# An attention and expert kernel: the expert units write into the score banks, the query turn comes earlier, the last gate follows the attention

## The chip, the cores and the metric

The kernel runs on one core of a Trainium2 chip. The metric is the device time of one launch in microseconds (us). An engine of the core works through its own queue in order: TensorE (PE, matrix products), VectorE (DVE), ScalarE (ACT), GpSimd (POOL) and SyncE (SP); transfers between memory and the core run on 16 DMA engines, issued here from the SP, POOL and ACT queues.

## The reference, cut to what matters

Attention with 16 query heads and one shared key and value head comes first; its output, with the heads side by side, are 3072 tokens of 1024 numbers. Then every token goes to one of 16 experts: a gate picks a group of four, a second gate one expert in the group.

```python
scores = scale * np.matmul(q, k.transpose(0, 1, 3, 2))      # q (8, 16, 384, 64), k and v (8, 1, 384, 64)
attn = np.exp(scores - max); attn = attn / attn.sum()
x = np.matmul(attn, v) as (3072, 1024)
g_idx = argmax(x @ w_group); e_idx = argmax(x @ w_expert[g_idx])
h = np.maximum(x @ w1[g, e], 0.0)                           # w1 (4, 4, 1024, 1024)
out = (g_w * e_w)[:, None] * (h @ w2[g, e])                 # softmax weights of the two picks
```

## The kernel before

All of the order is written by hand: each engine's queue holds its instructions in the order in which the program makes them, and the waits between engines follow from the tiles.

**Attention.** The work is cut into 48 groups `g`, six to a batch of 384 tokens (eight batches `b`), and into 24 pairs `p` of two groups. The loop at L418 runs 25 times; below, "stage p" is one turn of it. `r` is p mod 3: r = 1 is the stage in which the gate of the batch before is worked out. For a group, `scores(g, kt)` (L197) makes three tiles s on TensorE, and ScalarE turns each into pt with an exp. A score tile takes two PSUM banks; the pool `ps_s` has three such pairs of banks, and `side` (L77) hands out the same three to short-lived products. `values(g)` (L258) multiplies pt by v into a bank from `bank` (L72), which alternates between two single banks, mm0 and mm1. `pre_add` (L209) adds the three pt tiles on VectorE (two instructions). For the sums over keys, stages 1 to 7 use `sum_keys` (L232: a product kss on TensorE, and a turn krow on VectorE) and later stages `fold_keys` (L222: a turn and a reduce, both on VectorE). `invert` (L242) makes the product sm, and VectorE its reciprocal rc and the turned copy rinv. `weigh(g)` (L266) multiplies the values by rinv into xT on VectorE, GpSimd copies that to bf16 (xbf), and with a batch's last group SP stores x.

**Query turn.** `load_q(p)` (L82) loads a pair's q with four transfers from the SP queue, called in stage p - 3 behind the squares `stats_q` (L170) of that stage. `prep_q(p)` (L188) turns it on VectorE into qT; before, it is called in the middle of stage p - 1, ahead of the second group's scores.

**Gate.** `gate_a` (L280) makes the logits' parts gps on TensorE and copies them on ScalarE; `gate_b` (L290) makes the logits lps; `gate_math` (L304) copies them to L and works out the picks on VectorE, with one exp (ex, L315) on ScalarE; `gate_c` (L328) counts the picks (product cps; cnt and seven more small VectorE steps to gsel), reads the most used expert into a GpSimd register and issues the loads of that expert's w1 (two transfers) and w2 (one) from the POOL queue. Both have two buffers.

**Expert units.** For each batch the kernel computes all tokens with the most used expert: eight h units (L357, eight matmuls into hps, relu on ScalarE) and six y units (L366, eight matmuls into yps, a scaled copy on ScalarE into one of four y buffers, a store on SP). `fill(n)` (L407) places the next n units between the attention's products; 14 x 8 = 112 units in all, so that a unit that isn't placed early comes later. In stages from 7 on (`MOE_AT`), units stand in every stage. In the stages 10, 13, 16, 19 and 22 (and in 7) the gate's logits are put between the matmuls of a unit (`between`).

**The end.** After the loop come the last batch's gate, then with units between them: the list of the pairs of batch and expert that are left over (pe, pp, pl), the loads of such a pair (`load_pair`: w1 and w2 from POOL, xe from SP), the places of its tokens (pr, pick, pg), the gathering of its tokens (pb, px), a bound on the scores (sq, pq, bd, bdp, okf, oki: two reduces, two transposes on TensorE and five small steps), a register load on all engines that decides on a rare branch (rarei, L636), the rest of the units, and the pair's own two products (ph, py) and a scatter to the output.

Of the kernel before, what the change touches and what calls it, by code (L numbers as in the profile page):

```python
# [9 lines left out]
FP32 = mybir.dt.float32  # L10
BF16 = mybir.dt.bfloat16
I32 = mybir.dt.int32
U32 = mybir.dt.uint32
P = 128
ACTF = mybir.ActivationFunctionType
OP = mybir.AluOpType
# [5 lines left out]
def kernel(  # L22
# [49 lines left out]
    def bank(shape, dtype, name):  # L72
        at = turn_of[0]
        turn_of[0] = 1 - at
        return ps_m.tile(shape, dtype, tag="mm" + str(at), name=name)

    def side(shape, dtype, name):  # L77
        return ps_s.tile(shape, dtype, tag="s", name=name)
# [211 lines left out]
    def gate_b(b, between=False):  # L290
        ps = side([P, ST, 32], FP32, "lps")

        def logits(st):
            nc.tensor.matmul(out=ps[:, st, :], lhsT=part[b][:, st * P:(st + 1) * P], rhs=sel[:], start=True, stop=True)
        for st in range(ST):
            if between:
                inserts.append((0, lambda st=st: logits(st)))
            else:
                logits(st)
        if between:  # L300
            inserts.append((0, lambda: gate_math(b, ps)))
        return lambda: gate_math(b, ps)

    def gate_math(b, ps):  # L304
        L = pool.tile([P, ST, 5, 4], FP32, tag="L", bufs=1, name="L")
        nc.vector.tensor_copy(out=L[:].rearrange("p s a e -> p s (a e)"), in_=ps[:, :, 0:20])  # L306
        mx = pool.tile([P, ST, 5], FP32, tag="mx", bufs=1, name="mx")
        nc.vector.reduce_max(out=mx[:], in_=L[:], axis=AX)
        mxb = mx[:].unsqueeze(3).to_broadcast([P, ST, 5, 4])
        oh = pool.tile([P, ST, 5, 4], FP32, tag="oh", bufs=1, name="oh")  # L310
        nc.vector.tensor_tensor(out=oh[:], in0=L[:], in1=mxb, op=OP.is_ge)
        dl = pool.tile([P, ST, 5, 4], FP32, tag="dl", bufs=1, name="dl")
        nc.vector.tensor_sub(out=dl[:], in0=L[:], in1=mxb)  # L313
        ex = pool.tile([P, ST, 5, 4], FP32, tag="ex", bufs=1, name="ex")
        nc.scalar.activation(out=ex[:], in_=dl[:], func=ACTF.Exp)  # L315
        ohe = pool.tile([P, ST, 4, 4], BF16, tag="ohe", bufs=1, name="ohe")
        nc.vector.tensor_mul(out=ohe[:], in0=oh[:, :, 1:5, :], in1=oh[:, :, 0, :].unsqueeze(3).to_broadcast([P, ST, 4, 4]))
        ohe_t[b] = ohe
        smx = pool.tile([P, ST, 5], FP32, tag="smx", bufs=1, name="smx")
        nc.vector.reduce_sum(out=smx[:], in_=ex[:], axis=AX)  # L320
        ri = pool.tile([P, ST, 5], FP32, tag="ri", bufs=1, name="ri")
        nc.vector.reciprocal(out=ri[:], in_=smx[:])
        tt = pool.tile([P, ST, 4], FP32, tag="tt", bufs=1, name="tt")
        nc.vector.tensor_mul(out=tt[:], in0=ri[:, :, 1:5], in1=ri[:, :, 0:1].to_broadcast([P, ST, 4]))
        gv = gate_all[:, b * GE:(b + 1) * GE, :].rearrange("p (g e) s -> p s g e", g=G)
        nc.vector.tensor_mul(out=gv, in0=ohe[:], in1=tt[:].unsqueeze(3).to_broadcast([P, ST, 4, 4]))
# [26 lines left out]
    def moe_units(w1, w2, xb, gs, place, store):  # L353
        units = []
        state = {}

        def h_unit(fc):  # L357
            if fc == 0:
                state["h"] = pool.tile([P, FO, S], BF16, tag="hT", bufs=1, name="hT")
            ps = bank([P, CW], FP32, "hps")  # L360
            for ko in range(KO):
                nc.tensor.matmul(out=ps[:, 0:S], lhsT=w1[:, ko, fc * P:(fc + 1) * P], rhs=xb[:, ko * S:(ko + 1) * S], start=(ko == 0), stop=(ko == KO - 1))  # L362
                insert(ko)
            nc.scalar.activation(out=state["h"][:, fc, :], in_=ps[:, 0:S], func=ACTF.Relu)  # L364

        def y_unit(st, nh):  # L366
            cs = slice(nh * CW, (nh + 1) * CW)
            y = place(st, cs)
            ps = bank([P, CW], FP32, "yps")
            for fo in range(FO):  # L370
                nc.tensor.matmul(out=ps[:], lhsT=state["h"][:, fo, st * P:(st + 1) * P], rhs=w2[:, fo, nh * CW:(nh + 1) * CW], start=(fo == 0), stop=(fo == FO - 1))  # L371
                insert(fo)
            nc.scalar.activation(out=y, in_=ps[:], func=ACTF.Copy, scale=gs[:, st:st + 1])  # L373
            store(st, cs, y)

        for fc in range(FO):
            units.append(lambda fc=fc: h_unit(fc))
        for st in range(ST):
            for nh in range(2):
                units.append(lambda st=st, nh=nh: y_unit(st, nh))  # L380
        return units
# [36 lines left out]
    for p in range(NP + 1):  # L418
        b, r = divmod(p, RP)
        g = 2 * p  # L420
        live = p < NP
        busy = p >= MOE_AT
        if live:
            for kt in range(ST):
                scores(g, kt)
            stats_q(p)
            if p + 3 < NP:
                load_q(p + 3)
        else:
            fill(2)  # L430
        if p > 0 and p - 1 < MOE_AT:
            if r == 1 and b > 0:
                gate_a(b - 1)
            sum_keys(p - 1)
            if p > 1:
                values(g - 2)
            if r == 1 and b > 0 and not busy:
                math = gate_b(b - 1)
            if live:
                pre_add(g, 1)  # L440
                pre_add(g, 2)
            invert(p - 1)
            weigh(g - 2)
            if r == 1 and b > 0 and not busy:
                math()
        elif p > 0:
            invert(p - 1)
            values(g - 2)
            if live:
                pre_add(g, 1)  # L450
            weigh(g - 2)
            if live:
                pre_add(g, 2)
        else:
            pre_add(g, 1)
            pre_add(g, 2)
        if busy and live:
            if r == 1:
                gate_b(b - 1, between=True)
            fill(1)  # L460
            fold_keys(g)
            fill(1)
        if p + 1 < NP:
            prep_q(p + 1)
        if r == 2 and b + 1 < B:
            prep_k(b + 1)
            stats_k(b + 1)

        if live:
            for kt in range(ST):  # L470
                scores(g + 1, kt)
        if p == 0:
            values(0)
        else:
            values(g - 1)
        if live:
            pre_add(g + 1, 1)
            pre_add(g + 1, 2)
        if p > 0:
            weigh(g - 1)  # L480
        if r == 1 and b > 0 and not busy:
            gate_c(b - 1)
        if busy and live:
            assert not inserts
            if r == 1:
                gate_c(b - 1)
            fill(1)
            fold_keys(g + 1)
            fill(1)
            if r == 0 and p > MOE_AT:  # L490
                gate_a(b - 1)
            fill(p % 2)
        if r == 0 and b + 1 < B:
            load_kv(b + 1)

    last = B - 1
    fill(2)
    gate_a(last)
    fill(1)
    gate_b(last)()  # L500
    fill(1)
    gate_c(last)
    fill(1)


# [107 lines left out]
        fill(1)  # L613


    sq = pool.tile([P, 2], FP32, tag="sq", bufs=1, name="sq")
    nc.vector.reduce_max(out=sq[:, 0:1], in_=stat_q[:], axis=AX)
    nc.vector.reduce_max(out=sq[:, 1:2], in_=stat_k[:], axis=AX)
    pq = side([P, CW], FP32, "pq")
    for i in range(2):  # L620
        nc.tensor.transpose(out=pq[0:1, i * P:(i + 1) * P], in_=sq[:, i:i + 1], identity=ident[:])
    bd = pool.tile([1, 2], FP32, tag="bd", bufs=1, name="bd")
    nc.vector.reduce_max(out=bd[:], in_=pq[0:1, 0:2 * P].rearrange("p (a n) -> p a n", a=2), axis=AX)
    bdp = pool.tile([1, 1], FP32, tag="bdp", bufs=1, name="bdp")
    nc.vector.tensor_mul(out=bdp[:], in0=bd[:, 0:1], in1=bd[:, 1:2])
    okf = pool.tile([1, 1], FP32, tag="okf", bufs=1, name="okf")
    nc.vector.tensor_scalar(out=okf[:], in0=bdp[:], scalar1=60.0 * 60.0 / (4.0 * scale * scale), scalar2=None, op0=OP.is_le)
    oki = singles.tile([1, 1], I32, name="oki")
    nc.vector.tensor_copy(out=oki[:], in_=okf[:])
    raref = pool.tile([1, 2], FP32, tag="raref", bufs=1, name="raref")  # L630
    nc.vector.tensor_tensor(out=raref[:, 0:1], in0=small[0:1, 1:2], in1=small[0:1, 0:1], op=OP.is_gt)
    nc.vector.tensor_scalar(out=raref[:, 1:2], in0=okf[:], scalar1=-1.0, scalar2=1.0, op0=OP.mult, op1=OP.add)
# [29 lines left out]
    with rare_block:  # L662
# [7 lines left out]
      with tc.If(ok < 1):  # L670
# [42 lines left out]
          for b in range(B):  # L713
# [4 lines left out]
              nc.vector.tensor_copy(out=xg[:], in_=xT[b][:])  # L718
              nc.sync.dma_start(out=xb_dram[b], in_=xg[:])
              gate_a(b)  # L720
              gate_b(b)()
              for st in range(ST):
                  nc.sync.dma_start(out=outv[b, :, st, :], in_=zero[:])
          with tc.For_i(0, NPAIR, 1) as i:
# [32 lines left out]
```

## Time and profile before

| what | value |
|---|---|
| runs | 503.25 to 503.68 us, median 503.34 of 4 |
| the profiled execution's own time | 503.63 us |
| its span, first to last instruction | 502.1 us |
| TensorE, VectorE, ScalarE, GpSimd busy | 481.4, 334.4, 239.4, 67.2 us |
| weights loaded (queue q0) | 37.84 MB, 41.5% of the 16 engines' span |
| mean granted TensorE clock | 0.992 |

The profile is of one execution. A group's line names the source line, the engine, the operation and the tiles (out<-in), how often it ran, its busy time, the mean duration in ns, and the idle time before it with what ended that. A line of waits reads: who waited, for whom, us in total, times, longest. A line of the timeline reads: start, length, engine, line, operation, tiles, count, and in square brackets the idle time before it. A line of stretches reads: from:to, length, busy time and number of instructions of PE, PE's weight loads (PEld), DVE, ACT and POOL, then the granted clock, the busy share of the DMA engines and GB/s. Ends of matmuls are modelled, so times between units of TensorE are taken from start to start.

### The profile page before, as it was taken

The page shows a single profiled execution, that of the slowest core. Times are in us where ns is not written, and L with a number is a line of the kernel's source. Part 1 is how long each engine was busy: PE and PEld are TensorE (multiplying, and loading weights), DVE is VectorE, ACT ScalarE, POOL GpSimd, SP SyncE. Part 2 cuts the span into 40 slices and gives each one's busy share as a digit, 9 for nine tenths or more (in the row PEclk, how much of TensorE's full clock was granted, in tenths as well). Part 3 has the DMA queues.
Part 4 walks back from the last instruction along what each step waited for, and adds up shares of the span by engine and source line. Part 5 has one row for each costly group of instructions (what it writes and reads, how often), then busy time and mean ns, then how long its engine had stood idle before and what let it go on. Part 6 is the DMA issues. An engine that isn't in the chain of part 4 may idle for free. (4 is left out here: it accounts for less than half of the span.)

```text
span 502.1 us, 7022 instructions
## 1 busy us (share of the span) xinstructions
PE 481.4 (96%) x2623; PEld 203.4 (41%) x2623; DVE 334.4 (67%) x504; ACT 239.4 (48%) x341; POOL 67.2 (13%) x88
## 2 busy tenths in 40 slices
PE   8999999999999999999999999999999999998972
PEld 6333333344334343344334343344434343555540
DVE  4788688698775996598775987598766962422000
ACT  4755365536445546536445546446445542332321
POOL 1010020012011211013111211022101210110000
PEclk9999999999999999999999999999999999999997
DMA  9873629969975399439966399449931496599980
GB/s 129 75 102 44 129 23 211 191 124 166 208 191 109 44 212 215 141 63 163 211 173 126 49 209 196 138 85 176 201 126 64 66 210 175 135 243 257 215 210 12
DMA packets 148441, 73.05 MB, mean 146 GB/s; under 512 B 122651, under 2 KB 122651, under 8 KB 148400
## 3 DMA queue, kind: packets, MB, share of 16 engines
q0 software_dynamic: 19008, 37.84, 41.5%
q1 hardware_dynamic: 127792, 34.50, 33.6%
q8 instruction: 22, 0.36, 0.3%
q10 hardware_dynamic: 1600, 0.20, 0.3%
q14 instruction: 19, 0.16, 0.1%
HBM read 91.31 MB, written 19.40 MB: 221 GB/s over the span
## 5 line engine op out<-in xcount | busy, mean ns | idle before, releaser
L204 ACT ACTIVATE pt<-s 128x1024 f32<-128x1024 f32 x144 | 137.3, 1024 | 43.2 <-PE s L202 42.8
L202 PE MATMUL s<-qT,kT 64*128 64x512 f32 x576 | 137.1, 607 | 1.5 <-DVE L L306 0.7
L264 PE MATMUL o<-pt,v 128*64 128x512 f32 x576 | 133.6, 599 | 0.0
L362 PE MATMUL hps<-xbf,w 128*128 128x384 bf16 x512 | 89.6, 326 | 4.0 <-DVEq L662 2.0
L274 POOL CAST xbf<-xT 128x512 bf16<-128x512 f32 x48 | 44.3, 922 | 352.6 <-DVE xT L273 352.6
L371 PE MATMUL yps<-w,hT 128*128 128x512 bf16 x384 | 89.5, 380 | 0.0
L202 PEld LDWEIGHTS s<-qT,kT 64*128 64x128 f32 x576 | 51.5, 186 | 65.9 <-issue 54.7
L364 ACT ACTIVATE hT<-hps 128x384 bf16<-128x384 f32 x64 | 31.3, 491 | 87.7 <-PE hps L362 85.7
L264 PEld LDWEIGHTS o<-pt,v 128*64 128x64 f32 x576 | 37.2, 137 | 78.6 <-issue 66.5
L373 ACT ACTIVATE y<-yps,gsel 128x512 f32<-128x512 f32 x48 | 32.9, 686 | 72.9 <-PE yps L371 65.8
L362 PEld LDWEIGHTS <-w 128*128 128x128 bf16 x512 | 48.6, 99 | 46.0 <-issue 15.6
L212 DVE TENSOR_TENSOR presum<-pt 128x1024 f32<-128x1024 f32 x48 | 57.1, 1190 | 8.3 <-ACT pt L204 8.2
L216 DVE TENSOR_TENSOR presum<-presum,pt 128x1024 f32<-128x1024 f32 x48 | 58.6, 1221 | 3.3
L371 PEld LDWEIGHTS <-hT 128*128 128x128 bf16 x384 | 36.9, 100 | 51.6 <-issue 13.9
L251 DVE RECIPROCAL rc<-sm 128x32 f32<-128x32 f32 x24 | 8.5, 356 | 58.0 <-PE sm L249 57.3
L224 DVE STREAM_TRANSPOSE turn<-presum 128x1024 f32<-128x1024 f32 x34 | 42.1, 1238 | 0.4
L228 DVE TENSOR_REDUCE fold<-turn 128x32 f32<-128x1024 f32 x34 | 41.5, 1220 | 1.2
L273 DVE TENSOR_TENSOR xT<-o,rinv 128x512 f32<-128x512 f32 x48 | 32.9, 686 | 3.2 <-PE o L264 2.8
L253 DVE STREAM_TRANSPOSE rinv<-rc 128x1024 f32<-128x1024 f32 x24 | 29.9, 1245 | 0.8
L193 DVE STREAM_TRANSPOSE qT<-qraw 128x1024 f32<-128x1024 f32 (+1 forms) x25 | 29.8, 1191 | 0.3 <-DMA qraw<-in_q_dram 0.3
L172 ACT ACTIVATE junk<-qraw 128x1024 bf16<-128x1024 f32 x24 | 25.6, 1065 | 0.0
L315 ACT ACTIVATE ex<-dl 128x60 f32<-128x60 f32 x8 | 2.0, 253 | 30.6 <-DVE dl L313 30.6
(134 smaller groups left out, 186.7 us busy)
## 6 DMA issues: line engine op xcount, KB each, us to landing
w<-in_moe_w_dram POOLq DMA_DIRECT2D x18, 1024.0 KB, 13.5
w<-in_moe_w_dram POOLq DMA_DIRECT2D x9, 2048.0 KB, 23.8
out_dram<-y SPq DMA_DIRECT2D x48, 256.0 KB, 2.9
qraw<-in_q_dram SPq DMA_DIRECT2D x92, 128.0 KB, 3.9
x_bf<-xbf SPq DMA_DIRECT2D x8, 768.0 KB, 3.3
k<-in_k_dram SPq DMA_DIRECT2D x28, 48.0 KB, 2.6
v<-in_v_dram SPq DMA_DIRECT2D x8, 96.0 KB, 2.6
xe<-x_bf SPq DMA_DIRECT2D x1, 768.0 KB, 7.8
```

What stands on the lines that cost most here:

```text
L202: nc.tensor.matmul(out=ps[:, par, :], lhsT=kT[b][r, kt * P:(kt + 1) * P], rhs=qT[g][r, :], start=True, stop=True)
L204: nc.scalar.activation(out=t[:], in_=ps[:], func=ACTF.Exp, scale=scale)
L212: nc.vector.tensor_add(out=t[:], in0=pt[g, 0][:], in1=pt[g, 1][:])
L216: nc.vector.tensor_add(out=t[:], in0=t[:], in1=pt[g, 2][:])
L224: nc.vector.transpose(out=t[:], in_=presum[g][:].rearrange("p a n -> p (a n)"))
L228: nc.vector.reduce_sum(out=fold[p][:, ch, :], in_=t[:].rearrange("p (b i) -> p b i", i=32), axis=AX)
L264: nc.tensor.matmul(out=o_ps[g][64 * par:64 * par + 64, :], lhsT=v_sb[b][:, kt, :], rhs=pt[g, kt][:, par, :], start=(kt == 0), stop=(kt == ...
L273: nc.vector.tensor_mul(out=xT[b][:, cs], in0=o_ps[g][:], in1=rinv[p][:, ch * CW:(ch + 1) * CW])
L274: nc.gpsimd.tensor_copy(out=xbf[b][:, cs], in_=xT[b][:, cs])
L362: nc.tensor.matmul(out=ps[:, 0:S], lhsT=w1[:, ko, fc * P:(fc + 1) * P], rhs=xb[:, ko * S:(ko + 1) * S], start=(ko == 0), stop=(ko == KO - 1))
L371: nc.tensor.matmul(out=ps[:], lhsT=state["h"][:, fo, st * P:(st + 1) * P], rhs=w2[:, fo, nh * CW:(nh + 1) * CW], start=(fo == 0), stop=(fo ...
L373: nc.scalar.activation(out=y, in_=ps[:], func=ACTF.Copy, scale=gs[:, st:st + 1])
```

## The change

Six things change.

1. The units' products take their banks from `side` (the three pairs of score banks) and no longer from `bank`; the two single banks are left to the values.
2. The turn of the next pair's q stands at the start of the stage, behind the load of q and ahead of all other VectorE work of the stage, in stages 1 to 22; in stage 0 it stays.
3. The copy of the gate's logits out of PSUM is cut out of `gate_math` and stands, in the stages up to 6, ahead of `invert`.
4. In stage 1 the second group's scores stand ahead of `invert`.
5. From stage 7 on, `weigh` of the group before stands ahead of the second add of the new group.
6. Three units fewer stand ahead of the last gate (one at the end of stage 23, one in stage 24, one after the loop), and the bound on the scores, with its two transposes on TensorE, stands directly behind the last gate's `gate_c`, with two units behind it instead of none.

```diff
-            inserts.append((0, lambda: gate_math(b, ps)))
-        return lambda: gate_math(b, ps)
-
-    def gate_math(b, ps):
+            inserts.append((0, lambda: gate_math(b, gate_logits(ps))))
+        return lambda: gate_logits(ps)
+
+    def gate_logits(ps):
         L = pool.tile([P, ST, 5, 4], FP32, tag="L", bufs=1, name="L")
         nc.vector.tensor_copy(out=L[:].rearrange("p s a e -> p s (a e)"), in_=ps[:, :, 0:20])
+        return L
+
+    def gate_math(b, L):
...
-            ps = bank([P, CW], FP32, "hps")
+            ps = side([P, CW], FP32, "hps")
...
-            ps = bank([P, CW], FP32, "yps")
+            ps = side([P, CW], FP32, "yps")
...
             stats_q(p)
             if p + 3 < NP:
                 load_q(p + 3)
+            if 0 < p < NP - 1:
+                prep_q(p + 1)
         else:
-            fill(2)
+            fill(1)
         if p > 0 and p - 1 < MOE_AT:
-            if r == 1 and b > 0:
+            gate = r == 1 and b > 0
+            if gate:
                 gate_a(b - 1)
             sum_keys(p - 1)
             if p > 1:
                 values(g - 2)
-            if r == 1 and b > 0 and not busy:
-                math = gate_b(b - 1)
-            if live:
-                pre_add(g, 1)
-                pre_add(g, 2)
+            if gate and not busy:
+                logits = gate_b(b - 1)
+            pre_add(g, 1)
+            pre_add(g, 2)
+            if gate and not busy:
+                L = logits()
+            if p == 1:
+                for kt in range(ST):
+                    scores(g + 1, kt)
             invert(p - 1)
             weigh(g - 2)
-            if r == 1 and b > 0 and not busy:
-                math()
+            if gate and not busy:
+                gate_math(b - 1, L)
...
-        if p + 1 < NP:
-            prep_q(p + 1)
+        if p == 0:
+            prep_q(1)
...
-        if live:
+        if live and p != 1:
             for kt in range(ST):
                 scores(g + 1, kt)
...
         if live:
             pre_add(g + 1, 1)
+        if live and not busy:
             pre_add(g + 1, 2)
         if p > 0:
             weigh(g - 1)
+        if live and busy:
+            pre_add(g + 1, 2)
...
-            fill(p % 2)
+            if p < NP - 1:
+                fill(p % 2)
...
     last = B - 1
-    fill(2)
+    fill(1)
     gate_a(last)
     fill(1)
-    gate_b(last)()
+    gate_math(last, gate_b(last)())
     fill(1)
     gate_c(last)
+    sq = pool.tile([P, 2], FP32, tag="sq", bufs=1, name="sq")
+    nc.vector.reduce_max(out=sq[:, 0:1], in_=stat_q[:], axis=AX)
+    nc.vector.reduce_max(out=sq[:, 1:2], in_=stat_k[:], axis=AX)
+    pq = side([P, CW], FP32, "pq")
+    for i in range(2):
+        nc.tensor.transpose(out=pq[0:1, i * P:(i + 1) * P], in_=sq[:, i:i + 1], identity=ident[:])
+    fill(1)
+    bd = pool.tile([1, 2], FP32, tag="bd", bufs=1, name="bd")
+    nc.vector.reduce_max(out=bd[:], in_=pq[0:1, 0:2 * P].rearrange("p (a n) -> p a n", a=2), axis=AX)
...
+    nc.vector.tensor_copy(out=oki[:], in_=okf[:])
     fill(1)
...
-    sq = pool.tile([P, 2], FP32, tag="sq", bufs=1, name="sq")
-    nc.vector.reduce_max(out=sq[:, 0:1], in_=stat_q[:], axis=AX)
...
-    nc.vector.tensor_copy(out=oki[:], in_=okf[:])
```

The rare branch calls the gate's cut-out copy as well; nothing else changes there.

More of the change, by code (lines that the diff above doesn't have):

```diff
@@ L496 @@
     last = B - 1
-    fill(2)
+    fill(1)
     gate_a(last)
     fill(1)
-    gate_b(last)()
+    gate_math(last, gate_b(last)())
     fill(1)
     gate_c(last)
+    sq = pool.tile([P, 2], FP32, tag="sq", bufs=1, name="sq")
[7 more added lines that the diff above has]
+    nc.vector.reduce_max(out=bd[:], in_=pq[0:1, 0:2 * P].rearrange("p (a n) -> p a n", a=2), axis=AX)
+    bdp = pool.tile([1, 1], FP32, tag="bdp", bufs=1, name="bdp")
+    nc.vector.tensor_mul(out=bdp[:], in0=bd[:, 0:1], in1=bd[:, 1:2])
+    okf = pool.tile([1, 1], FP32, tag="okf", bufs=1, name="okf")
+    nc.vector.tensor_scalar(out=okf[:], in0=bdp[:], scalar1=60.0 * 60.0 / (4.0 * scale * scale), scalar2=None, op0=OP.is_le)
+    oki = singles.tile([1, 1], I32, name="oki")
+    nc.vector.tensor_copy(out=oki[:], in_=okf[:])
     fill(1)
@@ L613 @@
         fill(1)
-    sq = pool.tile([P, 2], FP32, tag="sq", bufs=1, name="sq")
-    nc.vector.reduce_max(out=sq[:, 0:1], in_=stat_q[:], axis=AX)
[L618 to L628, printed above, removed]
-    nc.vector.tensor_copy(out=oki[:], in_=okf[:])
     raref = pool.tile([1, 2], FP32, tag="raref", bufs=1, name="raref")
@@ L720 @@
               gate_a(b)
-              gate_b(b)()
+              gate_math(b, gate_b(b)())
               for st in range(ST):
```

## Prediction

> **What bounds the kernel now.** I read the page's engine table first, then TensorE's waits, then the order-of-time rows around each wait. Times are us from the start of the profiled execution.
>
> ```profile
> span 502.1 us, 7022 instructions
> PE 481.4 (96%) x2623; PEld 203.4 (41%) x2623; DVE 334.4 (67%) x504; ACT 239.4 (48%) x341; POOL 67.2 (13%) x88
> ```
>
> TensorE (PE) is the bound. Between 7.5 and 480 its units follow each other without gaps in most stages: three scores 2.77, a values group 2.73, an h unit 1.30, a y unit 1.73 (starts of consecutive units). So only TensorE's waits can be gained. This is their whole list, apart from the one before the first matmul:
>
> ```profile
> PE py L653 <- DMA w<-in_moe_w_dram: 3.7, 1, 3.7
> PE hps L362 <- DVEq L662: 2.0, 1, 2.0
> PE hps L362 <- DVE xT L273: 1.8, 3, 0.9
> ...
> PE sm L247 <- DVE krow L239: 0.9, 1, 0.9
> PE s L202 <- DVE L L306: 0.7, 1, 0.7
> PE s L202 <- DVE cnt L332: 0.5, 1, 0.5
> PE s L202 <- DVE rc L251: 0.3, 1, 0.3
> ```
>
> The list counts a gap from the modelled end of the matmul before. Measured start to start, a wait costs some 0.2 more, and some waits are not listed at all; I use start to start below. A unit that waits also reloads weights (0.1).
>
> **Stage 1 (15.57 to 26.74).** TensorE idles for krow (kss takes 2.00, elsewhere 1.00), then 0.45 for rc before a score. The change puts the scores of group 3 between kss and sm: 2.78 + 0.97 + 2.77 + 0.34 + 2.73 = 9.6 instead of 11.17. Its last score needs krow's bank, free at 20.2, and comes at 21.2; its q turn was done at 14.4, and its exps follow the squares on ScalarE (to 20.6) as now. The turn of the pair after fits in VectorE's (DVE's) idle 2.5 before krow. **Gain 1.6.**
>
> **Stages 4 and 5.** Two score waits, 0.91 for L at 61.9 and 0.65 for cnt at 68.5. Copying L before rc frees its bank at 60.0, so the first wait goes. But the gate's exp stands ahead of the scores' exps in ScalarE's (ACT's) queue, and waits for dl, which still follows rinv (1.35) and weigh (0.6):
>
> ```profile
> 63.50 0.25 ACT L315 ACTIVATE ex<-dl 128x60 f32<-128x60 f32 x1 [6.94 <-DVE dl L313]
> ```
>
> dl gains just L's 0.25. The exps then end at 64.4, 65.3, 66.25; the two adds follow at 65.4 and 66.7, weigh at 67.8, cnt ends at 68.6, where it ended at 69.10. Stage 5's third score waits for cnt's bank: **gain 0.5**, not 1.6. What is late next is the exp.
>
> **Stage 7.** Here the earlier turn meets a slow load. q of pair 8 is loaded in stage 5, from 72.5, beside 4 MB of weights. The last of its four transfers:
>
> ```profile
> L89 SPq DMA_DIRECT2D qraw<-in_q_dram x1: 8245/8245/8245, 85.1 to 85.1; - x1
> DMA to landing us min/median/max: 13.2/13.2/13.2
> ```
>
> It lands at 85.1 + 13.2 = 98.3. Before, the turn ran at 107.0. Now it stands right behind the weigh of 92.47, and krow, the adds, rc, rinv, weigh and L queue behind it:
>
> ```profile
> 92.47 0.68 DVE L273 TENSOR_TENSOR xT<-o,rinv 128x512 f32<-128x512 f32 x1
> 97.02 0.72 DVE L239 STREAM_TRANSPOSE krow<-kss 128x512 f32<-128x512 f32 x1 [3.87 <-PE kss L237]
> ...
> 102.43 0.21 DVE L306 COPY L<-lps 128x60 f32<-128x60 f32 x1
> ```
>
> The turn would run 98.4 to 99.6, so krow starts at 99.56, 2.54 late, and all behind it too. sm waits until 100.4 (0.9); the second h unit for rc's bank until 103.0 (0.6); the first score for L's bank until 105.2; the next two for the h units' relus, which follow ex on ScalarE, until 106.6 and 107.1. The scores end at 108.5 instead of 106.75. The second half saves the 0.5 that hps waited for xT at 111: stage 8 begins **1.3 later**. Had q been there, units on the score banks would not wait for xT (0.9 and 0.5) and I would count +1.3. Stages 10, 13, 16, 19 and 22 also turn earlier, but their q landed over 8 us before, in VectorE's idle time: no cost.
>
> **Stages 8 to 22.** A unit no longer waits for weigh (xT): 0.6 at 167, 0.3 at 223, 0.3 at 280. But weigh now stands ahead of the second add, and weigh needs the values group's end T. From T VectorE needs, start to start, weigh 0.60, add 1.15, the gate's eight count steps 1.65 and fold 2.49: sm can run at T + 6.0. TensorE is there after two h units and three scores, T + 5.4. Without the count it is 4.3, so plain stages have 1.1 to spare. Gate stages: 10 gains 0.1, 13 (three units) 0.3, 16 loses 0.3, 22 loses 0.6. **Sum -0.5.** The score banks themselves cost nothing as long as a unit is evacuated before the third score after it: that score begins 1.8 after the last unit's end, the evacuation ends 0.7 (h) or 0.8 (y) after it. Up to 408.7 the sum is 1.6 + 0.5 - 1.3 - 0.5 = **+0.3**.
>
> **The tail, TensorE.** Three units fewer stand before the last gate. (a) Stage 23: fold ends at 413.05 by the same chain (T = 408.8), sm would be due at 412.7: -0.45. (b) pq now stands directly behind cps. VectorE does gate math, the count and the gate sum first:
>
> ```profile
> 430.71 0.20 DVE L332 TENSOR_REDUCE cnt<-cps 128x16 f32<-128x48 f32 x1
> ...
> 432.23 0.20 DVE L350 TENSOR_REDUCE gsel<-gm 128x3 f32<-128x48 f32 x1
> ```
>
> cps ran at 430.19; the two sq reduces (0.3) would end 432.7: TensorE waits **2.5**; pe's wait of 0.3 goes. (c) The register load for the rare branch waited for the chain pq to rarei: 2.0. That chain is early now; what stays is xc's copy, four small steps (0.55) and the load (0.49) beside one y unit: 0.2 of wait, gain 1.8. The block's other steps (bd to oki, 0.9) run beside two y units. Together -0.45 - 2.5 + 0.3 + 1.8 = **-0.85**. The last product's hc is ready at 484.8 now, then at 484.8 + 0.85 - 0.3 = 485.35.
>
> **The tail, DMA.** It is busy from 432.5 to 487.7 (share 1.05 of 16 engines), so w2 of the extra pair lands by the total, not by its issue. The last gate's count, hence the first weight load, comes 4.7 + 0.3 earlier (three y-unit times of 1.73 less the 0.45 of wait); three more y stores fall into the stretch (0.26 MB at the 262 GB/s of the slices with stores is 1.0 each; the first load's start hides some, I take 0.8): landing at 487.67 - 5.0 + 2.4 = 485.1. Each load's buffer is free before the queue reaches it (the last about 460, some 10 us ahead). So py starts at about 485.4 instead of 487.81: **2.4**.
>
> The clock after the wait:
>
> ```profile
> 458.90:461.00 2.10, 0.08 (x2) 0.01 (x1) 1.26 (x8) 0.34 (x1) 0.00 (x0) 1.00 1.11 263
> 484.15:487.50 3.35, 0.00 (x0) 0.00 (x0) 0.00 (x0) 0.60 (x1) 0.00 (x0) 1.00 0.73 220
> 487.60:490.90 3.30, 3.09 (x8) 1.17 (x9) 0.00 (x0) 0.00 (x0) 0.00 (x0) 0.50 0.01 4
> ```
>
> Column PEclk (third from the end): after 3.66 idle, half clock; after 2.0, none. Seven of py's sixteen matmuls ran at 0.43 instead of 0.216: with under 1 us idle **1.55** comes back. For pq's 2.5 the rows bound the cost by nothing (2.0 idle) and 1.6 (3.66 idle); I take nothing, the nearer row.
>
> [...]
>
> **Sum.** 2.4 + 1.55 = 3.95 off the profiled 503.63 (span 502.1 and 1.5 around it) is 499.7; the median is 0.3 below that execution: **499.4 us**. All terms before the tail shift TensorE and the loads alike; they are in the 2.4.
>
> **Rivals.** (A) q of pair 8 doesn't hold VectorE (it lands sooner, or the turn isn't queued there): +2.6, **496.8**. Against it: the landing row. (B) The tail gives less: pq's gap trips the clock (1.6), or w2 lands 1.6 later because the loads' gaps and stores differ: **501.0**; over 3 us of idle the half clock is back too, 502.5. For it: the two ends of (a) to (c) and of the DMA meet within 0.3, so any further delay of either shows. (C) Slower: scores wait for banks that ScalarE has not emptied. A half stage has three scores behind units, 34 halves in all; the point from which it decides is an evacuation 1.9 after the unit's end. 0.15 lost in each half eats all; 0.3 gives **505.6**. For it: in gate stages the first unit's relu stands behind ex and ends 1.2 after its unit (stage 10). Against it: 0.7 and 0.8 for the last unit, whose bank is due soonest. (D) Nothing moves but places of waits: 503.3.
>
> **Numbers.** Forecast 0.58 (497.5 to 500.9), A 0.14, B 0.14, C 0.09, D 0.05. The range 496.4 to 501.9 takes in A and most of B, and leaves out C, D and B's far end. 0.2% (1.0 us) is about what a measurement here can tell from no change: faster 0.84, same 0.07, slower 0.09.
>
> **What would show it.** Stage 1 of 9.6 with no wait at sm; in stage 7 a DVE wait for qraw before qT, then 2.5 of delay, the scores waiting for L and the relus; no hps wait for xT; sm waiting for fold in stages 16, 22, 23; pq waiting 2.5 for sq; PEclk of 1.00 at py, whose wait is under 1. Wrong would be: score waits for hT or y in plain stages, py waiting 3 or more, a turn in stage 7 that starts before 98.

## The result and the profile after

The kernel after takes 501.32 us (median of 52 runs, 500.40 to 501.98), the kernel before 502.97 us in the same comparison (78 runs, 499.71 to 504.95): ratio 0.9974, 95% interval 0.9965 to 0.9982. Forecast were 499.4 us and a gain of 0.78%; it was 0.26% by the ratio and 1.65 us, 0.33%, by the medians. The profiled execution after took 501.75 us, 1.88 less than the one of before.

The head of the page, and TensorE's waits (who, for whom, us in total, times, longest):

```profile
span 500.2 us, 7021 instructions
PE 481.1 (96%) x2623; PEld 203.7 (41%) x2623; DVE 337.5 (67%) x504; ACT 238.9 (48%) x341; POOL 83.9 (17%) x88
```

```profile
PE pq L522 <- DVE sq L519: 2.3, 1, 2.3
PE sm L249 <- DVE fold L228: 1.7, 3, 0.6
...
PE s L202 <- DVE cnt L335: 1.3, 1, 1.3
PE s L202 <- DVE L L306: 0.7, 1, 0.7
PE sm L247 <- DVE krow L239: 0.7, 1, 0.7
PE sm L249 <- ACT hT L367: 0.5, 1, 0.5
PE s L202 <- DVE qT L193: 0.4, 1, 0.4
PE hps L365 <- DVE rc L251: 0.4, 1, 0.4
PE pb L629 <- DMA xe<-x_bf: 0.3, 1, 0.3
PE s L202 <- ACT hT L367: 0.3, 1, 0.3
PE s L202 <- ACT pt L204: 0.3, 1, 0.3
```

The two longest waits of before (py for w 3.7, hps for the register load 2.0) and all of hps for xT are gone. In their place stand pq's 2.3, sm for fold (sums of stages 10, 16 and 22), and small ones. The 0.5 of sm for hT, with stage 23's sums, is most likely fold too: sm starts 0.15 behind fold's end there, as at the other three, and the relu ended in between. The list adds up to 8.9 where that of before was 9.9: seen as waits, 1.0 is won. And a wait is not the whole price of a gap. The stretches around pq's gap, and py's at the end (from:to, length, busy us of PE, PEld, DVE, ACT, POOL, then the granted clock, DMA share, GB/s):

```profile
426.40:428.80 2.40, 0.13 (x2) 0.00 (x0) 2.12 (x14) 0.69 (x1) 0.12 (x1) 1.00 0.31 117
428.90:432.20 3.30, 3.30 (x9) 1.23 (x10) 0.84 (x4) 0.00 (x0) 1.15 (x2) 0.50 0.60 73
432.30:434.30 2.00, 2.00 (x11) 0.75 (x9) 0.00 (x0) 0.69 (x1) 0.00 (x0) 1.00 1.04 185
487.80:491.40 3.60, 3.60 (x20) 1.41 (x17) 0.00 (x0) 1.28 (x2) 0.00 (x0) 1.00 0.01 5
```

Behind the gap the clock stands at half (0.50) for 3.413 us, 428.85 to 432.26 (such a stretch is called a drop below): in the second stretch PE is busy throughout, with 9 matmuls, where the third has 11 in 2.0 us. py, on the other hand, now starts at 487.81 directly behind ph, at full clock (3.62 instead of 5.16): its start is the same as before, to the hundredth. The half clock has moved from py to pq; 1.54 was won at the one and 1.65 lost at the other (from pq's start to pe's 5.41, where runs 1 and 4 below, at full clock, have 3.76).

Where the time went, against the forecast's own steps (us, start to start, both profiled executions; plus is later):

| place | forecast | measured |
|---|---|---|
| start of the first score | 0 | +0.15 |
| stage 1 | -1.6 | -1.13 |
| stages 4 and 5 | -0.5 | -0.22 |
| stage 7 (q of pair 8) | +1.3 | +1.31 |
| stages 10, 13, 16, 22 | +0.5 | +0.61 |
| (a) sm in stage 23 | +0.45 | +0.55 |
| (b) pq's gap | +2.5 | +2.53 |
| (b) clock behind it | 0 | **+1.65** |
| pb waits for xe | 0 | +0.47 |
| (c) register load, what stays | 0.2 | 0.19 |
| ph's start to py | 4.44 | 3.57 |
| w2 lands at | 485.1 | 483.68 |
| py starts at | 485.4 | 487.81 |

The rows from the start to stage 22 make 1.02 more than forecast, (a) 0.10, the clock 1.65, xe 0.47, ph to py 0.87 less: 2.37 of the 2.41 by which py is late. The transfer was not the bound: py came 4.1 after w2's landing.

### The profile page after: what moved, and what is told of

Read it like the earlier page. It is cut to its first block, busy times and chain, and to the rows that moved or that the text cites. A ratio compares the mean times of both kernels' runs of the same rounds, so it can differ in the third digit from the quotient of the medians.

```text
span 500.2 us, 7021 instructions
## 1 busy us (share of the span) xinstructions
PE 481.1 (96%) x2623; PEld 203.7 (41%) x2623; DVE 337.5 (67%) x504; ACT 238.9 (48%) x341; POOL 83.9 (17%) x88
## 5 line engine op out<-in xcount | busy, mean ns | idle before, releaser
L274 POOL CAST xbf<-xT 128x512 bf16<-128x512 f32 x48 | 61.0, 1270 | 332.9 <-DVE xT L273 332.9
L374 PE MATMUL yps<-w,hT 128*128 128x512 bf16 x384 | 91.2, 384 | 0.0
```

Source lines behind the costliest of these rows:

```text
L274: nc.gpsimd.tensor_copy(out=xbf[b][:, cs], in_=xT[b][:, cs])
```

## The experiments

Theory: the half clock behind pq's gap took the most of what is missing; beside it, three orderings of the change cost time that can be had back (q of pair 8 early in stage 7, the add behind weigh, no unit ahead of pq). Rivals: the tail is bound by the last weight's transfer, so that such gains don't come through; or the parts of the change work otherwise than the table says. Ratios are to the kernel before on the same chip, with 95% intervals. Runs 1 to 4 were made on one chip, 5 to 7 on a second, 8 and the five-unit kernel of 7 on a third. Before's median was 503.23 on the first, 502.51 and 503.31 in two series on the second, 500.93 on the third, so a difference between runs on different chips is less sure than one on the same chip.

**1. Only the clock.** The kernel after with 36 matmuls of constants in the gap, whose result is never read.

```diff
+    idle = bank([P, CW], FP32, "idle")
+    for _ in range(36):
+        nc.tensor.matmul(out=idle[:, 0:P], lhsT=ones_bf[:], rhs=ones_bf[:], start=True, stop=True)
     pq = side([P, CW], FP32, "pq")
```

> The changed kernel with 36 idle matmuls (128x128, bf16, result never read) between cps and pq, so that the wait of 2.5 us stays but TensorE is busy in it. Theory G: the wait itself still costs 2.5 us, the granted clock stays at 1.00 behind it and the two y units behind pq take 3.5 us instead of 5.0: the time is that of the executions of the changed kernel without a drop, 500.2 to 500.7 us. Rival (the slow units behind pq are slow for another reason, such as their stores or banks): they still take 5.0 us, 501.3.

Measured: 500.09 us, 0.9932 (0.9916 to 0.9949). The same stretch as above:

```profile
428.90:432.20 3.30, 3.25 (x16) 1.56 (x16) 0.84 (x4) 0.69 (x1) 1.07 (x2) 1.00 0.68 78
```

Sixteen matmuls instead of nine, at full clock, and py 1.94 earlier (485.87), with pq at 428.80 instead of 428.88. Adding work that nobody needs made the kernel 1.2 us faster by the medians, and 0.4% (2.1 us) by the two ratios to before, whose intervals lie apart: the half clock is the cause of about that much, shown.

**2. Units in the gap.** Two units ahead of pq, none between pq and oki.

```diff
     gate_c(last)
+    fill(2)
     sq = pool.tile([P, 2], FP32, tag="sq", bufs=1, name="sq")
...
-    fill(1)
     bd = pool.tile([1, 2], FP32, tag="bd", bufs=1, name="bd")
...
     nc.vector.tensor_copy(out=oki[:], in_=okf[:])
-    fill(1)
```

> The changed kernel with the two units of the bound's block ahead of its transposes instead of behind them (the number of units is the same). Theory G (the gap behind the last gate): the 2.5 us wait of pq for sq lies under two y units (3.5 us), and the half clock of 3.4 us behind it (1.6 us) goes with it: ph starts 4.0 us earlier, py meets the landing of w2 (483.7) within 0.3 us; 501.3 - 4.0 = 497.3 us. Rival W (the end waits for the weights anyway): py starts no earlier than before, the gap only moves: 501.0 or more.

Measured: 499.64 us, 0.992 (0.9903 to 0.9937), 2.3 above what was expected. pe came 4.1 earlier (430.15), as it should; but xe, issued at 436.48, landed at 448.21 (11.7 later, beside the weights), pb waited 2.1 for it, and now the clock dropped there. The gap had moved on to the next dependence. That is the profiled execution, which at 501.69 is the slowest of the seven, 2.05 above their median; the others need not have had that drop.

**3. The turn of pair 8 late.** Only that one back in the middle of stage 7.

```diff
-            if 0 < p < NP - 1:
+            if 0 < p < NP - 1 and p != 7:
                 prep_q(p + 1)
...
-        if p == 0:
-            prep_q(1)
+        if p == 0 or p == 7:
+            prep_q(p + 1)
```

> The changed kernel with the turn of pair 8 alone back in the middle of stage 7. Theory Q (the turn waits for a load that lands at 97.2 and holds up VectorE's queue): stage 8 begins at 111.6 instead of 114.1, and the end comes 2.5 us earlier, 498.8 us. Rival B (stage 7 is slow because its units and scores share banks): stage 8 begins within 0.5 us of 114.1, 501 us.

Measured: 498.63 us, 0.9908 (0.989 to 0.9925): as expected to 0.2. Stage 8 begins 2.64 earlier, at 111.48. VectorE in stage 7, after and in this run (start, length, engine, line, operation, tiles, shapes, count, idle before):

```profile
97.23 1.25 DVE L193 STREAM_TRANSPOSE qT<-qraw 128x1024 f32<-128x1024 f32 x1 [5.76 <-DMA qraw<-in_q_dram]
98.40 0.67 DVE L239 STREAM_TRANSPOSE krow<-kss 128x512 f32<-128x512 f32 x1
```

```profile
95.71 0.72 DVE L239 STREAM_TRANSPOSE krow<-kss 128x512 f32<-128x512 f32 x1 [4.37 <-PE kss L237]
```

In the first, VectorE stands 5.76 in front of q, and krow follows; in the second krow runs as soon as kss is there. The forecast's step for stage 7 holds, on both sides.

**4. The second add ahead of weigh**, as it was before, in all stages.

```diff
-        if live and not busy:
+        if live:
             pre_add(g + 1, 2)
         if p > 0:
             weigh(g - 1)
-        if live and busy:
-            pre_add(g + 1, 2)
```

> The changed kernel with the second add of a group again ahead of weigh in the stages from 7 on. Theory F (weigh ahead of the add makes the sums late): the waits of sm for fold in the stages 16, 22 and 23 go, 1.7 us in all, and no other wait comes, because the units no longer need weigh: 499.6 us. Rival: with the add first the values' banks are late, and sm's gain is lost again: 501.3.

Measured: 498.65 us, 0.9906 (0.9889 to 0.9924), 1 better than expected. The waits of sm for fold are gone from the list, and the last gate's cps comes 2.6 earlier (423.72). In the tail pb now waits 1.2 for xe, where it waited 0.3; and besides pq's gap did not trip the clock in this profile. That makes a pair. First after, then this run:

```profile
428.88 0.58 PE L522 MATMUL pq<-ident,sq 128*1 128x128 f32 x2 [2.35 <-DVE sq L519]
429.25 5.11 PE L374 MATMUL yps<-w,hT 128*128 128x512 bf16 x16
```

```profile
426.26 0.38 PE L520 MATMUL pq<-ident,sq 128*1 128x128 f32 x2 [2.36 <-DVE sq L517]
426.48 3.62 PE L374 MATMUL yps<-w,hT 128*128 128x512 bf16 x16
```

The same gap, the same sixteen matmuls: 5.11 or 3.62. So it isn't the length of the gap alone that decides; section "What the runs showed" has what the traces tell of it.

**5. Parts of the change alone, on the kernel before.** The units on the score banks (item 1); the early turn (item 2); the tail (item 6).

```diff
-            ps = bank([P, CW], FP32, "hps")
+            ps = side([P, CW], FP32, "hps")
...
-            ps = bank([P, CW], FP32, "yps")
+            ps = side([P, CW], FP32, "yps")
```

> The kernel before with the units' products in the score banks, nothing else. My theory: the waits of hps for xT go (1.05 and 0.5 in stage 7, 0.7, 0.3 and 0.3 later), but in the stages 10 and 16 the sums of fold come no earlier and take some 0.6 of it back: stage 24 begins 1.5 to 2.0 us earlier and the time falls by as much, 503.0 to 501.2 us. Rival B (scores then wait for banks that ScalarE has not emptied): waits of s for hT or y, and 503 us or more.

Measured: 501.51 us, 0.9985 (0.9958 to 1.0013): inconclusive in time, since the interval takes in 1. The trace answers the question of rival C: no score waits for hT or y, hps no longer waits for xT, stage 8 begins 1.0 earlier. The banks cost no wait of a score.

```diff
             if p + 3 < NP:
                 load_q(p + 3)
+            if 0 < p < NP - 1:
+                prep_q(p + 1)
...
-        if p + 1 < NP:
-            prep_q(p + 1)
+        if p == 0:
+            prep_q(1)
```

> The kernel before with the query turn at the start of the stage, nothing else. Theory Q: VectorE waits for q of pair 8 in stage 7, weigh there comes 2.5 us late and the second h unit with it; stage 8 begins 2.0 to 2.5 us later, other stages gain 0.3 to 0.8 in all: 504.5 us. Rival: the turn fills VectorE's idle time everywhere, 502 to 503 us.

Measured: 502.57 us, 1.0005 (0.9979 to 1.0031), 1.9 below what was expected; no difference to before that can be told. TensorE did lose: without the score banks, units of stage 7 wait for xT behind the late VectorE, the clock drops there too (104.7), and stage 8 begins at 117.39, 3.4 later than before.

From its list of waits:

```profile
PE hps L362 <- DVE xT L273: 2.5, 1, 2.5
...
PE py L655 <- DMA w<-in_moe_w_dram: 1.2, 1, 1.2
```

But py's wait, 3.7 before, is 1.2 here, and the half clock behind it is gone (py 3.61 instead of 5.16): py starts 1.3 later than before and ends 0.2 earlier. A delay ahead of a wait is taken back at the wait, as far as the weight (here 1.3 later) allows. I had priced the delay and not the slack.

```diff
-    fill(2)
+    fill(1)
     gate_a(last)
...
     gate_c(last)
-    fill(1)
+    sq = pool.tile([P, 2], FP32, tag="sq", bufs=1, name="sq")
...
+    nc.vector.tensor_copy(out=oki[:], in_=okf[:])
```

> The kernel before with the new tail alone (three units fewer ahead of the last gate, the bound behind it). Theory G: pq waits 2.5 us and the clock halves behind it (1.6), the load of the rare register costs 1.8 less, pe 0.3 less; w2 lands some 3 us earlier and py no longer waits 3.7 us nor runs at half clock: py starts at 486.8 instead of 487.8 and takes 3.5 instead of 5.2: 500.5 us. Rival W: w2 lands no earlier and py waits as before, 503 us.

Measured: 500.05 us, 0.9965 (0.9942 to 0.9988): as expected. pq waits 2.3, the clock drops behind it at 428.5, py starts at 486.09 without a wait. Item 6 alone gives about what the whole change gives. What the other items win in stage 1 and lose in stage 7 and the gate stages is about even, as the table says.

**6. All three edits, 2 to 4, together.**

> The changed kernel with all three edits: two units ahead of pq, the turn of pair 8 in the middle of stage 7, the add ahead of weigh. If the three causes are separate, their gains add: 4.0 + 2.5 + 1.7 = 8.2 us, 493.1 us; w2 lands earlier with the last gate (2.5 + 1.7), so py meets it within some 0.5 us. Rival W: the weights' transfers take over as the bound at 483, and the time stays at 497.

Measured: 494.88 us, 0.9864 (0.9825 to 0.9902): 1.4% below before, 1.8 us above what was expected. It is pb again (start, length, engine, line, operation, tiles, count, idle before):

```profile
443.18 0.85 PE L626 MATMUL pb<-ident_bf,xe 128*128 128x128 bf16 x8 [2.07 <-DMA xe<-x_bf]
443.82 0.63 PE L374 MATMUL yps<-w,hT 128*128 128x512 bf16 x1
444.68 2.53 PE L374 MATMUL yps<-w,hT 128*128 128x512 bf16 x6 [0.22 <-issue]
```

**7. Cover for xe too.** Six units ahead of pb instead of four, on the kernel of 2 and then on that of 6; then five, on that of 6.

```diff
-    fill(4)
+    fill(6)
```

On the kernel of 2:

> The kernel after with two units ahead of pq and none behind it (as in the run with the units ahead of pq), and besides six instead of four units ahead of pb, two fewer left for the drain of the tail; the units are the same in number. Theory (the gain that the run with the units ahead of pq lacked, 499.64 us against an expected 497.3, lies in pb's wait of 2.1 us for the transfer of xe and in the half clock behind it, worth some 1.6 us): two units of 1.73 us stand in the place of that wait, no clock drop at pb, 499.64 - 2.1 to 499.64 - 3.7, so 496.0 to 497.5 us. Rival (the order of the tail is not what bounds: the second weight's transfer, or another wait, ends last): 499.4 to 499.9 us, with py waiting for that transfer.

Measured: 499.98 us, 0.9943 (0.9923 to 0.9963). The rival holds: the wait at pb is gone, and py waits instead, 2.1, for a weight that landed at 486.31; in run 2 it had landed at 483.96. It was issued 4.7 earlier and came 2.35 later. The profiled executions of this run and the next are each the slowest of their kernel, 1.8 and 2.0 above the medians, so the waits shown are those of a bad case.

On the kernel of 6:

> The kernel with all three edits (turn of pair 8 late, add ahead of weigh, two units ahead of pq), and six instead of four units ahead of pb. Theory: pb's wait of 2.1 us for xe and the half clock behind it go, 494.88 - 2.1 to 494.88 - 3.7; py came at 482.44 us without a wait there and the second weight had landed at 479.45 us, so up to 3.0 us can be had before that transfer ends last: 491.9 to 493.0 us. Rival (xe is asked for later too, or the transfer takes the place of the wait): 494.5 to 495.2 us.

Measured: 495.25 us, 0.985 (0.9816 to 0.9883). The same again: the weight at 481.65, where run 6 had it at 479.45. From 435 to 480 the DMA engines are full (share 1.11), and the clock falls behind the wait:

```profile
435.00:480.00 45.00, 43.77 (x311) 25.97 (x313) 4.40 (x13) 15.81 (x27) 2.24 (x3) 1.00 1.11 250
479.40:481.60 2.20, 0.00 (x0) 0.00 (x0) 0.00 (x0) 0.60 (x1) 0.00 (x0) 1.00 0.55 185
481.70:485.00 3.30, 3.08 (x7) 1.17 (x8) 0.00 (x0) 0.00 (x0) 0.00 (x0) 0.50 0.02 7
```

A unit moved ahead puts its store of y (0.26 MB, 1.05 us at 250 GB/s) in front of the weight; the counts fit that. In the first kernel of 7, 15 of the stores issued since 427 had landed when the weight did; in run 2 it was 12.

Five units, on the kernel of 6:

> The kernel with all three edits, and five instead of four units ahead of pb. In the run with four, pb waited 2.1 us for xe, with half clock behind it, and py came at 482.44 us with the second weight landed at 479.45 us; in the run with six, pb waited for nothing, but that weight landed at 481.65 us, 2.3 us after TensorE was ready for it, with half clock over py. Theory (in the tail the transfers go at a rate of their own, and each unit moved ahead puts one more store of y before the last weight, some 1.1 us): a wait of 0.4 us at pb and no half clock there, the weight at 480.5 us, a wait of some 1.3 us at py and no half clock there: 493.0 us, up to 494.6 us where the clock drops all the same. Rival (the weight's landing doesn't depend on the units ahead, the two profiles differ by chance): py without a wait, 492.0 us or below, or all three the same at 494.9 to 495.3 us.

Measured: 495.24 us, 0.9881 (0.9847 to 0.9915): not the 493.0 to 494.6 of the theory. Its profile shows what the theory asked for (pb 0.5, the weight at 480.92, py 1.7, no drop, py at 480.96, against 482.44 in run 6), and its span is 1.1 shorter than that of run 6. The medians don't show it. My error was to take a wait of one execution from a median of others: the profiled execution of run 6 (496.25) is 1.4 above its median, so most of its executions seem to go without the drop at pb.

**8. The last weight in halves.** Six units as in run 7, the last weight by two transfers, and py in the order of the halves.

```diff
-        nc.gpsimd.dma_start(out=w2[:], in_=w2f[bass.ds(e_reg, 1)].rearrange("a p k f -> (a p) k f"))
+        for a in range(2):
+            nc.gpsimd.dma_start(out=w2[:, 4 * a:4 * a + 4, :], in_=w2f[bass.ds(e_reg, 1)].rearrange("a p k f -> (a p) k f")[:, 4 * a:4 * a + 4, :])
...
+    pys = [side([P, CW], FP32, "py") for nh in range(2)]
+    for a in range(2):
+        for nh in range(2):
+            for fo in range(4 * a, 4 * a + 4):
+                nc.tensor.matmul(out=pys[nh][:], lhsT=hc[:, fo, :], rhs=w2c[:, fo, nh * CW:(nh + 1) * CW], start=(fo == 0), stop=(fo == FO - 1))
```

> The kernel with all three edits and six units ahead of pb, whose last weight (the second weight of the extra pair, 2 MB) is loaded by two transfers, four of the eight row blocks each, and whose last product does the first four blocks of both output halves before the last four. The bytes and the matmuls are the same. Theory (with six units it is the last weight's transfer that ends last, 2.3 us after TensorE was ready, and py at half clock follows, 5.22 instead of 3.62 us): py begins on the first half, which lands some 2 us or more before the second, and when the second lands about 481.7 us half of py is done; no half clock, the end of py at 483.5 us instead of 487 us: 495.25 - 3.3 = 492.0 us, up to 493.5 us where the halves land close together. Rival (the end isn't set by that transfer, or both halves land together as one did): 494.9 to 495.5 us.

Measured: 492.80 us (492.45 to 493.17), 0.9817 (0.9786 to 0.9847): the best version, and as expected.

TensorE's timeline at py:

```profile
479.19 1.89 PE L667 MATMUL py<-w,hc 128*128 128x512 bf16 x7
481.42 1.89 PE L667 MATMUL py<-w,hc 128*128 128x512 bf16 x8 [0.35 <-DMA w<-in_moe_w_dram]
```

The halves landed at 473.76 and 481.38. The first half of py runs while the second is under way; 0.35 of wait is left of 2.31, and no half clock. With the same units in the same places the end came 2.45 earlier in the median than with six units in run 7, on another chip, and 2.44 earlier than with five units on the same chip: the transfer was what ended last there.

## Why the prediction was wrong

The direction and the kind of change in each stage were right; the size was wrong by a factor of two and a half (medians) to three (ratio).

- **The step that failed** is the clock behind pq: "For pq's 2.5 the rows bound the cost by nothing (2.0 idle) and 1.6 (3.66 idle); I take nothing, the nearer row." It cost 1.65 in the profiled execution. Run 1 takes away the half clock and leaves the wait: 1.2 us come back in the median. The 501.0 of rival B, "pq's gap trips the clock", had 0.14 and is what happened (501.32); that the total met it so nearly is partly luck, since the other errors (1.6 late; 0.9 early, and 0.4 won behind py) largely offset each other. The row chosen was one throw of a die: in before, the gap of 2.02 left the clock at 1.00; in the first two kernels of run 5 the same gap, 2.03, did trip the clock (at 460.76 and 463.13). By 31 of after's 54 executions (below) the price should have been about 0.6 of 1.65, an estimate, not nothing. Rival B's half clock "over 3 us of idle" rests on the one row of 3.66; in the runs it came behind gaps from 2.03 on.
- **Stage 1**: 1.13 instead of 1.6. sm no longer waits long, but the third score of group 3 started at 21.75, by its wait in the bank of its own group's first score, whose exp ended at 21.70, and not in krow's, free since 20.4. "Its last score needs krow's bank" named the wrong one of three banks.
- **Stages 4 and 5**: 0.22 instead of 0.5. L's wait is gone, but ex begins at 62.53, and 63.50 less the 0.98 by which everything is ahead there is 62.52: it gained nothing of L's 0.25. The third score of stage 5 waits 1.3 for cnt.
- **Stage 7**: right to 0.01 as a sum, although q landed at 97.15 and not at 98.3; the h units' relus and L ended last, as foretold. Run 3 takes the term out, and with it 2.64. Rival A (that q doesn't hold VectorE) would have been this gain.
- **Stages 8 to 22** and (a): right to 0.1 each. Run 4 returns them.
- **(b) and (c)** as waits: right to 0.03.
- **Not forecast**: pb's 0.47 for xe. It was issued at 440.25 and landed at 450.19, 9.9 later beside the weights; I had followed the weights only.
- **ph to py**, 3.57 instead of 4.44: py's first four matmuls read only the first half of hc, and py started at 487.81 while the second relu ran from 488.01. An error to the other side; it hid 0.87 of the above.
- **DMA**: the weight landed 1.4 before the forecast. This made no difference, as TensorE was 4.1 later. In runs 7 and 8 it is the bound: there the rule "lands by the total, not by its issue" held, 4.7 earlier at the issue and 2.35 later at the landing.
- **Rival C** (scores waiting for banks that ScalarE hasn't emptied) fell: no such wait in plain stages; the one for hT is 0.3.
- **The base**: both sums were made against one execution. Before's executions lie in two groups, 23 of 78 below 501.5 and 55 above 502.3; the profiled 503.63 is in the upper. The gain between the profiles is 1.88, between the medians 1.65. What parts the two groups stays open.

## What to carry to other kernels

Price an idle stretch of TensorE as its length plus a chance of half clock behind it: here gaps of 1.26 us (after) and 1.7 us (run 7, five units) left the clock full, and of 12 gaps of 2.0 to 2.5 us 10 had half clock behind them, which cost 1.65 us in the profile after. So shorten such a gap or fill it, even with matmuls that nobody needs (run 1: 1.2 us faster). When a wait is removed, walk on to the next two dependences (here xe, then the last weight) with their own landing times before booking the gain; in a full queue the landing moved with what stood in front of it, not with the issue (run 7: issued 4.7 earlier, landed 2.35 later). And a delay ahead of a long wait costs nothing until the slack at the wait is used up (the early turn alone in run 5: stage 8 3.4 later, py's end 0.2 earlier).

## What the runs showed of the hardware

**The clock behind a gap of TensorE.** In the traces of before and after, each drop but the one cut off by the end is 3.413 us long (487.55 to 490.96, and 428.85 to 432.26), with matmuls of 512 columns 0.427 apart in it instead of 0.216. The gaps of 2 us and more in the 14 profiles, up to the last matmul, and two shorter ones:

| gap | us | clock behind it |
|---|---|---|
| s for cnt, after; py, five units of run 7 | 1.26; 1.7 | full |
| hps for the register load, before | 2.02 | full |
| the same, units on the score banks alone; early turn alone | 2.03; 2.0 | half |
| hps for xT, early turn alone | 2.45 | half |
| pq, after; run 3; tail alone | 2.35; 2.3; 2.3 | half |
| pq, run 4 | 2.36 | full |
| pb, runs 2 and 6 | 2.1; 2.07 | half |
| py, run 7 with six units, on the kernels of 2 and 6 | 2.10; 2.31 | half |
| py, before | 3.66 | half |

The length alone doesn't tell 2.35 from 2.36. In the clock records of before and after, the drops of one execution begin whole multiples of 3.413 apart (before: 487.55 and 497.79, 3 of them; after: 428.85 and 493.70, 19). Counted back in such steps, before's gap, 458.93 to 460.95, is cut at 460.25 into 1.32 and 0.70: full clock. After's, 426.53 to 428.88, has 2.32 within the step that ends at 428.85: half. Py's gap in before has 3.40 within the step that ends at 487.55: half. Run 4's is cut into 1.26 and 1.10: full. That the cut is what decides is my reading of these four gaps; no run tested it.

Of after's 54 executions with a listed clock, 31 have a mean of 0.992 or less (one drop takes 0.0034 off the mean); I take these for the ones with a drop behind pq. The median times of these and of the rest are 501.61 and 500.76: 0.85 apart, where one drop cost 1.65 in the profile. What makes up the rest stays open.

**GpSimd's cast took 1.54 us where it started beside an add of two tiles, 0.61 elsewhere.** Its mean went from 922 to 1270 ns with the change, and back to 942 with the second add ahead of weigh. Cast by cast there are two lengths in all three traces: 609 to 616 ns, or 1535 to 1542 ns where it starts while an add of two tiles runs, without an exception; of the long ones there are 16 of 48 before, 34 after and 17 in run 4. The line of after, then of run 4 (count, busy us, mean ns, idle before):

```profile
L274 POOL CAST xbf<-xT 128x512 bf16<-128x512 f32 x48 | 61.0, 1270 | 332.9 <-DVE xT L273 332.9
```

```profile
L274 POOL CAST xbf<-xT 128x512 bf16<-128x512 f32 x48 | 45.2, 942 | 347.3 <-DVE xT L273 347.3
```

Behind weigh, the cast runs beside the add (two operands from SBUF) instead of the turn (one), beside which 11 of before's casts took 0.61. What of the add slows it is not shown. I take it to cost no time here: GpSimd is busy 17% of the span, and TensorE's list has no wait for xbf.
